# New tables for the attention loop and the MLP's list of a fused transformer block

## The chip, the cores and the metric

The kernel runs on one core of a Trainium2 chip. The core has TensorE (PE, with its weight loads as PEld), VectorE (DVE), ScalarE (ACT), GpSimd (POOL), and SyncE (SP), which here only issues transfers; sixteen DMA engines move the data. The metric is the device time of one launch in microseconds (us). Each time comes from several launches; one further launch is profiled.

## The reference

One block of a conditioned transformer, on 2048 tokens of width 640. A condition vector gives six modulation vectors (shift `s`, scale `c`, gate `g`, for two halves of the block). Everything is fp32.

```
mod = silu(c) @ w_mod                       # 6 vectors of 640
h = layernorm(x) * (1 + ca) + sa
q, k, v = h @ wqkv                          # 32 heads of 20
scores = q @ k.T * 20**-0.5                 # a query sees its own and the 255 tokens before
x = x + ga * (softmax(scores) @ v) @ wo
h = layernorm(x) * (1 + cb) + sb
x = x + gb * (gelu(layernorm(h) @ w1 + b1) @ w2 + b2)    # 640 -> 1536 -> 640
```

## The kernel before

**Splits.** Nearly every operand of a large product is held as a high and a low part (`hi`, `lo`), and a product of two of them is three matmuls: hi x hi, hi x lo, lo x hi. The high part is a rounding copy, the low part the difference of the value and its high part. Each copy and each difference is an instruction on DVE, ACT or POOL, and the tables say on which.

**Three stages.** A prologue normalizes the first 1024 tokens and makes the first q and k. Then comes a loop of steps `t`, 0 to 143, in which attention is computed while the remaining projections (q, k, v of the other heads and tokens) run beside it as filler for TensorE. Then comes the MLP with the output projection `wo` and the second and third layernorm of each group of 128 tokens (`bg`, 0 to 15), written as one explicit list.

**A step of the loop.** A quad is four heads; there are 8 quads and two halves of 1024 tokens, 16 in all, of 8 query blocks each. Step `t` computes the scores `s` of one query block (for their row maxima only), and, 11 steps later in the loop, `e`: the scores once more, transposed, with the maxima subtracted inside the product. DVE masks `e` and `s` and takes the maximum (`nm`); ACT takes the exponential of `e` (`pt`), POOL masks `pt`; two steps later TensorE multiplies `pt` with v (`o`), and ACT copies the result (`oT`). The maxima of a quad are turned and split at step 8k (`m_rows`: a transpose `pm`, two ACT instructions `mt` and `mhi`, one POOL difference `mlo`) and stored by SP as two rows each (`mhi`, `mlo`) into `qbuf`; `e` needs them from step 8k + 3 on. So rows written at step 64 are needed at step 67, those of step 80 at 83, and those of step 88 at 91.

**Four slots.** Behind the scores and the exponential each step has four slots, h = 0 to 3; a time like 64.25 means step 64, slot 1. All engines get their instructions in the order of the program. SP is one queue: a transfer that waits for a buffer, for data or for an earlier transfer to land holds up all transfers behind it.

**What fills the slots.** A unit is one q, k or v product of 128 features and 512 tokens: 15 matmuls, then an evacuation of hi and low part (or a copy of v and its four transposes, called an aside, since it needs a bank of its own). `UNITS` orders the units. `lay_units` spreads their matmuls over the steps, some 7.35 a step, with `EXTRA[t]` more or fewer at step t, and `LEAST` 4 at least while a unit lasts. `LOV` lists the units whose low part goes to DVE instead of POOL. `EARLY` and `AFTER` move the weight splits and the asides of a unit. A finished unit's q or k is written to DRAM by SP in the next step (`rows_out`: `q_scr`, `k_scr`), and read back for a quad into `qbuf` and `kbuf` by `rows_in`, not before two steps behind its last unit. Then there are, as time intervals: `MODS` for the modulation vectors of the second half (five loads `wm`, five additions on DVE), `WOS` for the output weights (`wor` loads, splits), `RS` for the sums of the softmax (a load `rd`, a reciprocal on DVE, a store `r_scr`), `LNS` and `HIA` for the layernorm of the tokens of the second half, `W1S` and `LATE_AT` for the first MLP weights and the last v, and `PREP`, `PREPS`, `PREPE`, `AHEAD` for splitting the MLP weights. For the latter, a load of 128 x 640 is issued `AHEAD` steps before, at `PREP` ACT makes the high part, a slot later the engine of `PREPE` the low part, and `PREPS` steps after `PREP` SP stores both.

`SUMS_LAST` lists steps in which the copy of `o` comes behind the exponential, `WHOLE` steps in which the maximum is one instruction instead of two. `WARM` puts matmuls without a use into a few steps. `TAIL_AT`, `TAIL0`, `PER` place the first token groups of the output projection into the last steps.

**The MLP's list.** `PLAN` is a list of words. A number n stands for the next n groups of three matmuls; each other word is a named operation, of `ops`. `w2hj` loads the w2 tile of step j into one of three buffers (`W2B`), `ghj` and `gl_j` split the activation, `load.Na`, `load.Nb` and `load.Nc` load attention output, reciprocal sums and x of token group N, `xrcm` loads a residual, `xbcm` adds its bias, `clcm` closes an output tile, `stcm` stores it, `a..`, `b..`, `e..` are sums and gelus of the first product. A residual load `xr` takes the buffer of a stored tile, so it waits until that store has landed. `MOVE` names the engine of each copy and difference of the list: `d` DVE, `a` ACT, `p` POOL.

The evacuation of rows, and the reading back, in the loop:

```python
                    for kind in range(2):
                        t = max([t, due - 8 * NSLOT + LAG + 8] + [over_at.get((kind, j, c2), -9) + 2 for j in js])
                        put(max(t, 0), 3, lambda half=half, quad=quad, kind=kind, c2=c2: rows_in(half, quad, kind, c2))
```

and the weights of the MLP:

```python
            later(at, lambda: nc.scalar.copy(hi, src))
            later(at + 0.25, lambda: e.tensor_tensor(lo, src, f32(hi), ALU.subtract))
            later(at + hold, store)
```

Of the kernel before, what the change touches and what calls it, by code (L numbers as in the profile page):

```python
# [99 lines left out]
e201 xr02 y1.4a 1 sa1.5a gh1 y1.4b 1 sa1.5b xr03 y1l.4 sa1.5c m0.5 w00.6 gl_1 load.7c x0.5a m1.5 w01.6 1 xr04 om.7  # L100
w02.6 1 sb0.5 sb1.5a w03.6 sr00 1 sb1.5b sb1.5c oh.7 rd.8 w04.6 x0.5b 1 ol.7 add0.6 n2.5 x1.5a sa0.6 1 xb00 x1.5b
p102 w10.6 xs.5 xb01 load.8a y0.5a 1 load.8c xb02 w11.6 y0.5b xb03 1 y0l.5 w12.6 raw.5a y1.5a xb04 1 t1.5 y1.5b
y1l.5 w13.6 raw.5b 1 t1h.5 w14.6 ri.8a t3.5 1 add1.6 1 ri.8b t1l.5 t2.5 x0.6a sa1.6a 1 a202 w00.7 x0.6b w2h4 e202 1
t2h.5 sa1.6b t4.5 load.8b sa1.6c gh2 w01.7 m0.6 1 gl_2 w02.7 m1.6 p103 x1.6a w03.7 load.9a w04.7 t2l.5 1 add0.7 1
sb0.6 om.8 w10.7 1 sa0.7 oh.8 w11.7 load.9b sb1.6a 1 x1.6b sb1.6b ol.8 xs.6 w12.7 1 w13.7 om.9 sb1.6c load.9c v000 1
a203 load.10b w14.7 e203 1 z000 add1.7 n2.6 1 sa1.7a oh.9 k000 w00.8 gh3 w2h5 y0.6a ol.9 gl_3 w01.8 1 y0.6b load.10a
sa1.7b y0l.6 w02.8 k100 1 sa1.7c raw.6a w03.8 k200 k300 t1.6 v100 1 k400 p104 w04.8 t1h.6 1 add0.8 t1l.6 y1.6a w10.8
z100 1 m0.7 w11.8 1 y1.6b m1.7 w12.8 y1l.6 1 sb0.7 raw.6b sb1.7a x0.7a a204 1 x0.7b sb1.7b w13.8 e204 v200 sb1.7c
sa0.8 1 z200 w14.8 n2.7 gh4 1 ss00 t3.6 gl_4 sr01 add1.8 x1.7a 1 om.10 x1.7b w2h6 y0.7a xs.7 t2.6 1 y0.7b load.10c
sa1.8a w00.9 load.11b p105 y0l.7 1 oh.10 sa1.8b t2h.6 y1.7a sa1.8c raw.7a 1 m0.8 t4.6 w01.9 t1.7 1 t2l.6 w02.9 y1.7b  # L110
t1h.7 m1.8 1 t1l.7 w03.9 y1l.7 1 sb0.8 raw.7b sb1.8a w04.9 a205 v001 1 t3.7 sb1.8b e205 add0.9 1 z001 t2.7 gh5 w10.9
1 sb1.8c th00 t2h.7 w11.9 w2h7 t2l.7 t4.7 w12.9 n2.8 k201 1 gl_5 sa0.9 th01 w13.9 ol.10 1 tl00 w14.9 a600 1 load.11a
add1.9 1 sa1.9a w00.10 sa1.9b 1 sa1.9c w01.10 k001 1 om.11 tl01 w02.10 1 oh.11 rd.12 w03.10 1 w04.10 1 k101 a700 1
add0.10 ol.11 1 b500 w10.10 a500 e500 1 k301 v101 load.11c w11.10 1 k401 z101 v201 w12.10 1 ri.12a z201 w13.10 a400
ri.12b 1 sr02 e400 w14.10 1 ss01 gh6 add1.10 1 gl_6 load.12b w00.11 a300 1 e300 w01.11 w2h8 1 v002 w02.11 z002 1
w03.11 k002 k202 a601 1 k102 w04.11 v102 k302 1 add0.11 1 k402 w10.11 z102 1 w11.11 1 v202 w12.11 z202 1 ss02 w13.11
sr03 a701 1 b501 w14.11 a501 1 e501 add1.11 4 a401 1 e401 1 gh7 1 a301 gl_7 1 e301 1 w2h9 v003 1 z003 1 a602 k203 1
k003 1 k103 1 v103 k303 1 z103 k403 2 a702 1 v203 b502 1 z203 a502 e502 2 ss03 sr04 1 a402 1 e402 1 gh8 1 gl_8 1
a302 1 e302 w2h10 2 a603 4 v004 z004 2 a703 1 k004 b503 k104 1 a503 e503 1 k304 k204 1 k404 v104 1 a403 v204 z104 1
z204 e403 1 gh9 1 a303 sr05 1 gl_9 e303 1 ss04 w2h11 2 a604 2 v005 1 z005 1 k005 k205 k105 1 k305 1 v105 k405 a704 1  # L120
z105 v205 1 b504 1 a504 z205 e504 2 a404 ss05 1 e404 1 gh10 1 a304 w1h10 gl_10 w1h11 1 e304 1 w2h12 2 a605 6 a705 1
b505 1 a505 e505 3 a405 1 e405 1 gh11 1 a305 w1h12 w1h13 1 gl_11 e305 x0.8a w2h13 gh12 1 x0.8b gl_12 1 cl00 x1.8a 1
x1.8b load.12a cl01 xs.8 y0.8a cl02 1 st00 y0.8b st01 1 y0l.8 st02 cl03 1 w2h14 gh13 y1.8a st03 cl04 1 y1.8b m0.9 1
# [1726 lines left out]
```

## Time and profile before

| | us |
|---|---|
| median of 3 runs | 974.69 |
| lowest, highest | 973.71, 974.96 |
| the profiled execution | 974.81 |
| its span, first to last instruction | 973.1 |

The profile lists busy time by engine, the granted clock of TensorE, the transfers, and for each instruction the idle time of its engine just before it with what ended it (its releaser). In a row of a timeline the first number is the start, the second the duration of the rows merged in it, both in us; `x3` counts them. In a view of waits the numbers are total us, times, and the longest. In a table of windows each engine has its busy time and its number of instructions, in the order PE, PEld, DVE, ACT, POOL; behind them stand the granted clock, the share of the DMA engines' time in use, and GB/s. `out<-in` names what an instruction writes and reads. Times in the views count from the start of the span.

### The profile page before, as it was taken

How to read it: one execution, taken by the hardware profiler on the slowest of the kernel's cores; microseconds unless marked ns; L12 is line 12 of the kernel's file. 1: busy time of each engine (PE TensorE's matmuls, PEld its weight loads, DVE VectorE, ACT ScalarE, POOL GpSimd, SP SyncE). 2: the span in 40 equal slices, each digit the busy share in tenths (PEclk: the TensorE clock that was granted, in tenths of full speed). 3: DMA queues.
4: the chain of work that ended last, by engine and by line, in shares of the span. 5: the costliest groups of instructions: out<-in, count | busy, mean ns of one | idle time of the engine just before them, and what ended most of it. 6: DMA issues, size and time to landing. Idle time of an engine off the chain costs nothing. (4 is left out here: it accounts for less than half of the span.)

```text
span 973.1 us, 20083 instructions
## 1 busy us (share of the span) xinstructions
PE 937.3 (96%) x7693; PEld 739.0 (76%) x7693; DVE 656.9 (68%) x1099; ACT 416.3 (43%) x738; POOL 491.8 (51%) x662
## 2 busy tenths in 40 slices
...
GB/s 309 96 213 214 295 289 324 267 224 264 264 310 264 228 278 218 288 118 149 215 165 171 80 88 332 172 190 173 206 245 274 278 165 244 210 169 180 97 288 162
DMA packets 109039, 212.01 MB, mean 218 GB/s; under 512 B 9840, under 2 KB 43088, under 8 KB 107408
## 3 DMA queue, kind: packets, MB, share of 16 engines
...
q8 instruction: 61, 1.00, 0.4%
...
## 5 line engine op out<-in xcount | busy, mean ns | idle before, releaser
L191 POOL TENSOR_SCALAR_AFFINE_SELECT pt<-pt 128x512 f32<-128x512 f32 x192 | 132.0, 687 | 126.9 <-ACT pt L191 115.0
L191 PE MATMUL out<-ghi,w 128*128 128x512 f32 x480 | 170.8, 397 | 1.8 <-DMA w<-w_scr 1.8
L191 ACT ACTIVATE pt<-e 128x1024 f32<-128x1024 f32 (+1 forms) x120 | 133.8, 1115 | 62.8 <-DVE e L191 62.0
L191 DVE TENSOR_REDUCE nm<-s 128x1 f32<-128x256 f32 (+4 forms) x193 | 156.8, 841 | 4.4
L191 PE MATMUL e<-qbuf,kbuf 62*128 62x128 f32 (+2 forms) x773 | 112.9, 330 | 14.6 <-ACT pt L191 9.7
L191 PEld LDWEIGHTS e<-qbuf,kbuf 62*128 62x128 f32 x773 | 80.9, 186 | 54.1 <-ACT pt L191 28.0
L191 PE MATMUL pp<-hhi,w_hi 128*128 128x512 f32 x265 | 115.3, 435 | 0.1
L191 DVE COPY_PREDICATED e<-mask_t,e 128x512 f32<-128x512 uint32 x96 | 66.6, 693 | 68.4 <-PE e L191 61.3
L191 PE MATMUL s<-kbuf,qbuf 60*128 60x256 f32 (+2 forms) x728 | 107.3, 304 | 4.0 <-DVE nm L191 1.5
L191 PE MATMUL pp<-hlo,w_hi 128*128 128x512 f32 x265 | 108.5, 410 | 1.3 <-POOL hlo L191 1.3
L191 PE MATMUL pp<-hhi,w_lo 128*128 128x512 f32 x265 | 105.6, 399 | 0.0
L191 PEld LDWEIGHTS out<-ghi,w 128*128 128x128 f32 x480 | 90.3, 188 | 19.2 <-ACT ghi L191 2.0
L191 PE MATMUL o<-pt,vbuf 128*32 128x128 f32 x2688 | 100.9, 279 | 0.0
L191 PEld LDWEIGHTS s<-kbuf,qbuf 60*128 60x128 f32 x728 | 88.3, 187 | 13.9 <-DVE nm L191 5.7
L191 PE MATMUL out<-glo,w 128*128 128x512 f32 x240 | 94.1, 392 | 0.2 <-DVE glo L191 0.2
L191 PE MATMUL P<-yhi,w1s 128*128 128x512 f32 x264 | 89.3, 391 | 1.1 <-DVE u L191 1.1
L191 DVE COPY_PREDICATED s<-mask_t,s 128x512 f32<-128x512 uint32 x112 | 77.1, 689 | 15.1 <-PE s L191 14.8
L191 POOL TENSOR_TENSOR w_lo<-wraw,w_hi 128x128 fp32r<-128x128 f32 (+1 forms) x166 | 75.8, 488 | 20.8 <-ACT w_hi L191 20.8
L191 ACT COPY oT<-o 128x128 f32<-128x128 f32 x128 | 33.9, 265 | 121.1 <-PE o L191 117.8
L191 PEld LDWEIGHTS o<-pt,vbuf 128*32 128x32 f32 x2688 | 67.7, 110 | 15.6 <-issue 3.1
L191 PEld LDWEIGHTS pp<-hhi,w_hi 128*128 128x128 f32 x265 | 49.9, 188 | 21.8 <-issue 12.3
L191 PE MATMUL wo<-wo_h,ot_hi 128*128 128x320 f32 x256 | 62.3, 326 | 0.1
...
## 6 DMA issues: line engine op xcount, KB each, us to landing
...
```

The lines of the kernel that those rows point to most:

```text
L191: return self.tc.keep_in_program_order(op(*args, **kw))
```

## The change

All lists of numbers named above are replaced, and nothing else: no function, shape, buffer or product changes. In the loop's tables:

```diff
-UNITS = ((0, ...), (1, 'q10', 'k00', 'q00', 'k10', 'q01', 'k11', 'k01', 'q11', 'v0', ...))
+UNITS = ((0, ...), (1, 'q10', 'k00', 'q00', 'k10', 'q01', 'k01', 'k11', 'q11', 'v0', ...))
-LNS = [-10.25, -3.75, -1.0, -1.5, 0.75, -0.5, 0.0]
-LOV = [1, 8, 12, 17, 18, 23, 24, 25, 35, 37, 43, 44, 47, 52, 55]
-HIA = [0, 1, 4, 5, 6, 7]
+LNS = [-10.75, -3.75, -1.0, -1.5, 0.75, -1.0, 0.0]
+LOV = [1, 8, 15, 17, 18, 24, 25, 28, 31, 35, 37, 43, 44, 47, 52, 55]
+HIA = [1, 2, 3, 5, 6, 7, 9]
-MODS = [[8.5, 18.25], [18.5, 27.25], [69.75, 79.0], [58.25, 67.25]]
-WOS = [86.5, 93.25, 98.75, 108.5, 111.75, 114.5, 118.5]
-W1S = [124.25, 122.25]
-RS = [[78.75, 80.5], [82.5, 86.75]]
+MODS = [[8.75, 18.75], [19.0, 27.25], [66.75, 77.25], [56.25, 65.25]]
+WOS = [86.0, 93.25, 98.25, 108.5, 111.75, 113.75, 117.5]
+W1S = [126.0, 121.5]
+RS = [[78.75, 80.25], [82.5, 84.75]]
-WARM = {(135, 0): 3, (136, 0): 4, (114, 3): 8, (120, 3): 1}
+WARM = {(135, 0): 2, (136, 0): 1, (114, 3): 8}
-PREP = [10.25, 14.5, 16.5, 25.0, 26.75, 29.25, 38.25, 39.75, 42.0, 49.75, 52.5, 54.5, 63.75, 65.5, 67.5, 75.0, 77.0, 78.5]
-PREPS = [0.75, 2.0, 1.5, 1.5, 1.5, 0.75, 1.0, 1.75, 2.0, 1.5, 1.5, 2.0, 1.5, 2.5, 0.5, 1.25, 2.0, 1.75]
-PREPE = 'ppppppppdpdppppppp'
-AHEAD = 4.0
+PREP = [9.0, 15.5, 16.25, 24.0, 26.75, 29.0, 38.0, 39.75, 41.75, 49.5, 52.25, 54.25, 64.25, 66.25, 67.25, 74.5, 77.25, 78.5]
+PREPS = [0.5, 1.75, 1.75, 1.75, 1.5, 0.5, 1.25, 1.75, 2.0, 1.5, 1.5, 2.0, 1.5, 2.0, 0.5, 1.25, 2.5, 1.75]
+PREPE = 'pppppddddppppppppp'
+AHEAD = 5.25
```

`EXTRA` has new values for about half of its steps. Worked out through `lay_units`, the products of a step change in 30 of 100 steps, mostly by one or two; the larger ones are step 21 (3 to 13), step 22 (15 to 2), step 33 (7 to 11), step 29 (10 to 8) and steps 47 and 48 (6 and 5 to 4 and 7). `EARLY` changes for 15 units, `AFTER` moves the asides of v1 to steps 74 and 75 (from 73 and 74), of v2 and v3 to 98 and 102 (from 97 and 101) and of the modulation vectors by one to three steps. `SUMS_LAST` loses four steps and gains five, `WHOLE` loses five and gains seven. `TAIL_AT` and `LATE_AT` change in single entries by a quarter step or so.

`PLAN` is written anew in the part where token groups and the first products run together, and nearly word for word the same where only MLP products are left. An example, the stretch at the last chunk of 512 tokens:

```diff
-w2h37 1 gh36 cl20 1 gl_36 cl21 st20 1 cl22 st21 1 cl23 st22 1 cl24 w2h38 gh37 st23 1 gl_37 st24 1 xr30 1 xr31 1 xr32 1 w2h39 gh38 1 gl_38 1 xr33 2 xr34 1 xb30 w2h40
+w2h37 1 gh36 cl20 1 gl_36 st20 1 cl21 1 cl22 st21 1 cl23 w2h38 st22 1 cl24 st23 1 gh37 st24 gl_37 1 xr30 1 xr31 1 gh38 w2h39 1 gl_38 2 xr32 1 xr33 1 gh39 w2h40 xr34
```

`MOVE` names another engine for 153 of its 326 words, for instance:

```diff
-'gh5': 'a', 'oh.6': 'p', 'gh14': 'p', 'v000': 'a', 'k102': 'p', 'gh36': 'a', 'gl_36': 'p'
+'gh5': 'a', 'oh.6': 'd', 'gh14': 'd', 'v000': 'p', 'k102': 'd', 'gh36': 'a', 'gl_36': 'd'
```

More of the change, by code (lines that the diff above doesn't have):

```diff
@@ new lines @@
+AFTER = {0: 1, 4: 3, 5: 2, 6: 1, 7: 1, 8: 1, 9: 1, 10: 2, 11: 1, 12: 3, 14: 1, 15: 3, 20: 1, 21: 1, 22: 1, 23: 3, 32: 1, 34: 2, 35: 1, 36: 1, 38: 1, 39: 3, 40: 4, 43: 2, 1: 1, 57: 2, 50: 4, 37: 1, 46: 2, 29: 1, 3: 1, 41: 1, 53: 2, 51: 2, 56: 2, 13: 1, 58: 3, 49: 1, 54: 1, 16: 1, 44: 1, 59: 1, 2: 1}
+SUMS_LAST = [14, 18, 23, 25, 26, 29, 33, 34, 42, 46, 59, 61, 64, 79, 80, 83, 85, 87, 88, 91, 92, 94, 100, 101, 105, 106, 107, 109, 110, 117, 121, 122, 123, 126, 128, 129, 130, 132, 133, 134, 135, 136, 137]
@@ L69 @@
-WOS = [86.5, 93.25, 98.75, 108.5, 111.75, 114.5, 118.5]
-W1S = [124.25, 122.25]
-RS = [[78.75, 80.5], [82.5, 86.75]]
+MODS = [[8.75, 18.75], [19.0, 27.25], [66.75, 77.25], [56.25, 65.25]]
+WOS = [86.0, 93.25, 98.25, 108.5, 111.75, 113.75, 117.5]
+W1S = [126.0, 121.5]
+RS = [[78.75, 80.25], [82.5, 84.75]]
 TOMID = 109
-WARM = {(135, 0): 3, (136, 0): 4, (114, 3): 8, (120, 3): 1}
-LATE_AT = [106.25, 106.25, 106.75, 108.5, 110.75, 111, 113.75]
+WARM = {(135, 0): 2, (136, 0): 1, (114, 3): 8}
+LATE_AT = [106.25, 106.5, 106.75, 108.5, 110.75, 111, 113.5]
@@ L100 @@
[L100 to L123, printed above, removed]
-st04 1 gl_13 m1.9 2 om.12 w2h15 gh14 1 sb0.9 load.13b sb1.9a oh.12 1 gl_14 xr10 1 ol.12 xr11 1 sb1.9b xr12 y1l.8
@@ L150 @@
-a715 1 b515 1 a515 e515 3 a415 1 e415 1 gh35 1 gl_35 1 a315 1 e315 w2h37 1 gh36 cl20 1 gl_36 cl21 st20 1 cl22 st21 1
-cl23 st22 1 cl24 w2h38 gh37 st23 1 gl_37 st24 1 xr30 1 xr31 1 xr32 1 w2h39 gh38 1 gl_38 1 xr33 2 xr34 1 xb30 w2h40 1
-gh39 xb31 1 gl_39 xb32 3 gh40 w2h41 1 xb33 gl_40 1 xb34 3 gh41 w2h42 1 gl_41 4 w2h43 gh42 1 gl_42 4 w2h44 gh43 1
-gl_43 4 gh44 w2h45 1 gl_44 4 gh45 w2h46 1 gl_45 4 gh46 w2h47 1 gl_46 4 gh47 1 gl_47 5 cl30 1 cl31 st30 1 cl32 st31 1
-cl33 st32 cl34 st33 st34
+load.6a w1h02 w2h1 w2h2 w2h3 w1h03 1 load.6b 1 m0.4 1 p100 x0.4a oh.5 1 m1.4 ol.5 1 x0.4b sb0.4 1 sb1.4a w1h04 x1.4a
@@ new lines @@
+ra00 1 ra01 w00.5 w01.5 x1.4b sb1.4b w02.5 p101 w03.5 a200 1 e200 w04.5 1 gh0 sb1.4c add0.5 1 sa0.5 gl_0 n2.4 w10.5
+w11.5 w12.5 w1h05 om.6 a201 y0.4a load.6c 1 load.7a y0.4b e201 xs.4 y0l.4 w13.5 xr00 1 oh.6 gh1 load.7b xr01 y1.4a 1
+ol.6 xr02 y1.4b y1l.4 w14.5 1 add1.5 gl_1 xr03 1 sa1.5a sa1.5b w00.6 m0.5 x0.5a sa1.5c w01.6 load.7c 1 m1.5 w02.6
+sr00 1 sb0.5 w03.6 sb1.5a 1 p102 xr04 sb1.5b w04.6 x0.5b sb1.5c 1 add0.6 xb00 om.7 x1.5a sa0.6 1 n2.5 load.8a w10.6
+x1.5b 1 xb01 xs.5 rd.8 y0.5a oh.7 w11.6 y0.5b 1 ol.7 xb02 y0l.5 w12.6 xb03 a202 y1.5a w13.6 raw.5a e202 load.8c 1
@@ new lines @@
+y1.5b t1.5 gh2 w14.6 y1l.5 1 raw.5b xb04 1 gl_2 t1h.5 add1.6 1 w2h4 t1l.5 w00.7 x0.6a t3.5 w01.7 ri.8a x0.6b 1
+sa1.6a x1.6a ri.8b w02.7 p103 t2.5 1 x1.6b sa1.6b xs.6 m0.6 w03.7 sa1.6c 1 t4.5 w04.7 load.9a 1 t2h.5 load.8b m1.6 1
+t2l.5 1 add0.7 sb0.6 w10.7 sb1.6a 1 v000 sa0.7 sb1.6b w11.7 z000 a203 1 om.8 e203 sb1.6c w12.7 1 gh3 k000 load.9b
+oh.8 k100 w13.7 w2h5 gl_3 1 n2.6 w14.7 1 ol.8 add1.7 y0.6a sa1.7a 1 om.9 k200 1 load.9c sa1.7b w00.8 load.10b y0.6b
+oh.9 v100 p104 w01.8 y0l.6 w02.8 sa1.7c ol.9 1 k300 raw.6a w03.8 load.10a y1.6a w04.8 k400 z100 1 t1.6 1 y1.6b m0.7
@@ new lines @@
+1 v200 1 add0.8 1 m1.7 w10.8 w2h6 y1l.6 w11.8 sb0.7 raw.6b x0.7a sb1.7a w12.8 a204 x0.7b t3.6 w13.8 sb1.7b w14.8
+e204 sa0.8 sb1.7c 1 z200 gh4 add1.8 x1.7a t2.6 1 ss00 n2.7 x1.7b sa1.8a load.10c gl_4 w00.9 om.10 xs.7 p105 y0.7a
+sr01 t2h.6 w01.9 y0.7b w02.9 1 y0l.7 oh.10 load.11b w03.9 sa1.8b raw.7a sa1.8c y1.7a ol.10 1 y1.7b t1.7 w04.9 m0.8
+load.11a 1 t1h.7 1 t1l.7 y1l.7 m1.8 1 raw.7b 1 add0.9 sb0.8 1 t3.7 sb1.8a w10.9 t1h.6 1 th00 t2.7 t1l.6 a205 w11.9
+w2h7 t2h.7 sb1.8b t4.7 w12.9 t2l.6 e205 w13.9 sb1.8c t2l.7 w14.9 gh5 t4.6 1 sa0.9 th01 gl_5 add1.9 1 tl00 n2.8
@@ new lines @@
+w00.10 tl01 1 w01.10 a600 1 sa1.9a w02.10 sa1.9b 1 w03.10 om.11 1 w04.10 1 add0.10 v001 oh.11 rd.12 1 sa1.9c ol.11
+w10.10 a700 1 a500 w11.10 z001 1 b500 load.11c ri.12a w12.10 e500 k001 1 k201 ri.12b w13.10 k101 1 v101 w14.10 k301
+z101 1 add1.10 k401 1 load.12b w00.11 1 a400 v201 w01.11 e400 z201 1 gh6 w02.11 a300 1 sr02 gl_6 e300 w03.11 ss01 1
+w04.11 w2h8 1 add0.11 1 w10.11 a601 1 v002 w11.11 z002 1 k002 k202 w12.11 k102 1 v102 k302 w13.11 1 z102 k402 w14.11
+2 add1.11 v202 1 a701 z202 1 a501 1 b501 sr03 1 e501 1 ss02 1 a401 1 e401 1 gh7 1 gl_7 1 a301 v003 1 z003 e301 w2h9
@@ new lines @@
+1 cl00 x1.8a 1 x1.8b load.12a cl01 xs.8 y0.8a 1 cl02 st00 y0.8b st01 1 y0l.8 st02 cl03 1 gh13 w2h14 cl04 y1.8a st03
+1 gl_13 st04 1 m0.9 1 y1.8b m1.9 2 y1l.8 w2h15 om.12 x0.9a 1 sb0.9 load.13b oh.12 sb1.9a 1 x0.9b ol.12 sb1.9b xr10 1
+sa0.10 sa1.10a x1.9a xr11 1 gh14 x1.9b sb1.9c xs.9 w00.12 sa1.10b w2h16 w01.12 w02.12 gl_14 n2.9 w03.12 w04.12 gh15
+y0.9a xr12 1 sa1.10c y0.9b load.12c gl_15 1 y0l.9 load.13a 1 y1.9a 1 m0.10 1 xr13 y1.9b xr14 m1.10 1 xb10 w2h17 1
+gh16 xb11 sb0.10 gl_16 1 sb1.10a y1l.9 1 sb1.10b sa0.11 sb1.10c x0.10a sa1.11a 1 x0.10b sa1.11b sa1.11c 1 n2.10
@@ new lines @@
+w2h18 gh17 x1.10a 1 xb12 x1.10b load.13c gl_17 xs.10 y0.10a add0.12 1 y0.10b w10.12 y0l.10 1 om.13 y1.10a xb13
+w11.12 m0.11 1 y1.10b xb14 oh.13 load.14b w12.12 w2h19 y1l.10 w13.12 m1.11 x0.11a gh18 w14.12 1 sb0.11 add1.12 ol.13
+1 sb1.11a sa0.12 1 sb1.11b sa1.12a 1 gl_18 load.14a sa1.12b w00.13 1 sb1.11c x0.11b w01.13 gh19 w2h20 sa1.12c 1
+n2.11 gl_19 w02.13 1 x1.11a 1 x1.11b load.14c xs.11 w03.13 om.14 1 load.15b oh.14 w04.13 1 add0.13 ol.14 y0.11a gh20
+w2h21 1 y0.11b w10.13 load.15a 1 y0l.11 gl_20 y1.11a w11.13 y1.11b m0.12 1 ra10 w12.13 y1l.11 1 m1.12 w13.13 1
@@ new lines @@
+w14.13 gh21 w2h22 ra11 1 add1.13 x0.12a sb0.12 1 x0.12b sa0.13 w00.14 sa1.13a sb1.12a 1 sb1.12b x1.12a gl_21 sa1.13b
+1 x1.12b xs.12 w01.14 1 sa1.13c sb1.12c w02.14 gh22 w2h23 1 gl_22 om.15 n2.12 w03.14 1 w04.14 1 oh.15 add0.14 y0.12a
+1 ol.15 y0.12b w10.14 y0l.12 1 load.15c w11.14 gh23 w2h24 1 gl_23 w12.14 1 w13.14 1 w14.14 1 add1.14 y1.12a 1 y1.12b
+m0.13 w00.15 w2h25 y1l.12 1 m1.13 w01.15 x0.13a sb0.13 1 sb1.13a x0.13b sa0.14 w02.15 sb1.13b p110 sa1.14a 1 sb1.13c
+sa1.14b w03.15 cl10 sa1.14c 1 n2.13 st10 w04.15 cl11 1 add0.15 st11 x1.13a 1 x1.13b xs.13 y0.13a 1 y0.13b w10.15
@@ new lines @@
+6 a712 1 a512 1 b512 1 e512 2 a412 1 e412 1 gh32 1 a312 sh14 gl_32 1 e312 1 w2h34 2 a613 6 a713 1 a513 1 b513 1 e513
+2 a413 1 e413 1 gh33 1 a313 sh15 gl_33 1 e313 1 w2h35 2 a614 6 a714 1 a514 1 b514 1 e514 2 a414 1 e414 1 gh34 1 a314
+gl_34 1 e314 1 w2h36 2 a615 6 a715 1 a515 1 b515 1 e515 2 a415 1 e415 1 gh35 1 gl_35 1 a315 1 e315 w2h37 1 gh36 cl20
+1 gl_36 st20 1 cl21 1 cl22 st21 1 cl23 w2h38 st22 1 cl24 st23 1 gh37 st24 gl_37 1 xr30 1 xr31 1 gh38 w2h39 1 gl_38 2
+xr32 1 xr33 1 gh39 w2h40 xr34 1 gl_39 xb30 1 xb31 3 gh40 w2h41 1 xb32 gl_40 1 xb33 3 gh41 w2h42 xb34 1 gl_41 4 gh42
```

59 lines of the change are left out of this document (23 added, 36 removed).

## The prediction

> **What bounds the kernel now.** The page's busy table comes first, then busy time by stage.
>
> ```profile
> PE 937.3 (96%) x7693; PEld 739.0 (76%) x7693; DVE 656.9 (68%) x1099; ACT 416.3 (43%) x738; POOL 491.8 (51%) x662
> ```
> ```profile
> 50.00:500.00 450.00, 437.28 (x4600) 324.70 (x4600) 334.99 (x464) 249.62 (x472) 274.11 (x404) 1.00 0.78 241
> 500.00:600.00 100.00, 90.63 (x1080) 72.53 (x1081) 77.44 (x133) 48.89 (x86) 57.42 (x73) 0.97 0.51 158
> 600.00:900.00 300.00, 297.33 (x1449) 247.27 (x1448) 196.26 (x365) 78.03 (x123) 125.02 (x141) 1.00 0.62 213
> 900.00:973.10 73.10, 67.24 (x295) 54.74 (x293) 18.17 (x28) 13.05 (x20) 14.06 (x13) 1.00 0.53 183
> ```
>
> TensorE is the bound. After the start it idles 12.7 us in the loop of 128 score steps (450.00 - 437.28), 9.4 us where attention runs out, 2.7 us in the MLP's middle and 5.9 us at the end. The tables move work and take none of it away, so they can win only these idles, and what a lowered clock costs beside them. The view of waits, for PE alone, names who ended them:
>
> ```profile
> PE e L191 <- ACT pt L191: 9.7, 15, 2.0
> PE e L191 <- DMA qbuf<-mlo: 3.4, 3, 2.1
> PE out L191 <- DMA w<-w_scr: 1.8, 2, 1.6
> ```
>
> Two of the three are transfers, 5.2 us together. The timeline of PE gives the places, the longest first (idle before the row and its releaser in brackets):
>
> ```profile
> 304.08 0.40 PE L191 MATMUL pp<-hhi,w_lo 128*128 128x512 f32 x1
> 304.31 0.40 PE L191 MATMUL pp<-hhi,w_hi 128*128 128x512 f32 x1
> 306.83 0.77 PE L191 MATMUL e<-qbuf,kbuf 62*128 62x256 f32 x3 [2.12 <-DMA qbuf<-mlo]
> ```
>
> The wait at 306.83 costs more than its 2.12 us. Busy time in short windows, the granted clock third from the end:
>
> ```profile
> 300.00:306.80 6.80, 4.71 (x43) 3.14 (x41) 5.14 (x7) 2.82 (x4) 3.32 (x3) 1.00 0.96 318
> 307.50:310.30 2.80, 2.80 (x35) 2.07 (x33) 1.86 (x3) 0.18 (x2) 0.00 (x0) 0.50 1.01 352
> 311.00:316.00 5.00, 5.00 (x59) 3.72 (x58) 2.61 (x5) 3.76 (x9) 3.78 (x5) 1.00 0.20 78
> 938.00:942.00 4.00, 3.84 (x17) 3.20 (x18) 0.00 (x0) 1.44 (x3) 1.17 (x1) 1.00 0.72 285
> ```
>
> Behind it the clock is 0.50 for at least 2.80 us (307.50 to 310.30) and at most 4.2 (306.80 to 311.00). Half of that is lost: 1.4 to 2.1 us. Behind the wait at 938 (below) it stays 1.00.
>
> **The row transfers (step 67).** mhi and mlo are the rows of score maxima of one quad, written at step 64 and needed by e at step 67. SP's issues ahead of the late one:
>
> ```profile
> 295.93 0.33 SPq L191 DMA_DIRECT2D prep<-in_w  x1
> 298.29 1.13 SPq L191 DMA_DIRECT2D kbuf<-k_scr  x2
> 299.47 0.39 SPq L191 DMA_DIRECT2D wraw<-in_wqkv  x1
> 299.90 0.94 SPq L191 DMA_DIRECT2D q_scr<-stage  x2
> 300.94 0.53 SPq L191 DMA_DIRECT2D qbuf<-mhi  x1
> 301.74 1.35 SPq L191 DMA_DIRECT2D qbuf<-mlo  x1
> ```
>
> Sizes follow from shapes: a row transfer 32 x 128 floats, 16 KB; each kbuf 60 x 2 x 512, 240 KB; a prep load 128 x 640, 320 KB, its store twice that; xr 128 x 512, 256 KB. mlo's 16 KB hold e until 306.83, 5.1 us after the issue began, while the DMA share is 0.96: it stands behind what was issued just before. UNITS swaps k1's and k0's second chunk, so quad 0's k0 is complete at step 59 instead of 61 and the kbuf pair goes out at step 61 instead of 63. There SP waits for k0's write to land, with step 62's k_scr writes queued behind it; nothing of these is due before step 64, so 0. AHEAD 5.25 moves the prep load from 63.5 to 62.0. That takes 800 KB out of the run-up; at 318 GB/s, 2.6 us. PREP 64.25 also puts prep's low part on POOL behind mlo instead of ahead of it:
>
> ```profile
> L191 POOL TENSOR_TENSOR prep<-prep 128x640 fp32r<-128x640 f32 x16 | 25.6, 1598 | 10.8 <-ACT prep L191 10.8
> ```
>
> so mlo itself can be ready 1.6 us earlier. Of the 2.12 us the bytes alone cover all. I take the whole idle and 1.6 us of clock: **-3.7 us** (bounds 0 and -4.2).
> The Trainium skill (TensorE: Matmul & The Clock Gate, "Part 1: The HAM clock gate") says that the clock is halved after an idle window of about 3.4 us. By that rule 2.12 us would halve nothing, this term would be -2.1 and the time 971.0; the rows show the halving right behind 2.12 us, so I give the rule 0.02, inside the forecast's chance.
>
> **Step 91.** Here SP itself is late with the rows:
>
> ```profile
> 404.09 0.52 PE L191 MATMUL e<-qbuf,kbuf 62*128 62x128 f32 x5 [1.06 <-DMA qbuf<-mlo]
> ```
>
> ```profile
> 394.32 1.77 SPq L191 DMA_DIRECT2D kbuf<-k_scr  x2
> 396.19 0.58 SPq L191 DMA_DIRECT2D r_scr<-rd  x1
> 397.74 1.59 SPq L191 DMA_DIRECT2D q_scr<-stage  x2
> 399.42 0.58 SPq L191 DMA_DIRECT2D qbuf<-mhi  x1
> 401.47 0.55 SPq L191 DMA_DIRECT2D qbuf<-mlo  x1
> ```
>
> Before the kbuf pair stand four wor loads. WOS starts them half a step earlier (86.0) and RS stores r_scr two steps earlier (84.75). mlo is issued at 301.74 in step 64 and at 401.47 in step 88: 4.2 us a step, so half a step is some 2.1 us, an estimate. Against 1.06 us I take **-0.9** (0 to -1.1).
>
> **The last chunk.**
>
> ```profile
> 928.23 2.22 SPq L191 DMA_DIRECT2D xr<-x_scr  x3
> 930.50 0.44 SPq L191 DMA_DIRECT2D w<-w_scr  x1
> ```
> ```profile
> 938.16 0.47 PE L191 MATMUL out<-ghi,w 128*128 128x512 f32 x1 [1.63 <-DMA w<-w_scr]
> ```
>
> The w2 tile of 930.50 reaches its matmul at 938.16. Three residual loads are issued ahead of it; in the new list two are (xr32 follows w2h39), and w2h38 goes ahead of three stores instead of two. One xr less is 0.26 MB at the 285 GB/s around 938, 0.9 us, and its issue 0.7 us of 2.22. But cl21 to cl24 come one group later, and their stores free the buffers that xr waits for; and w2 has only three buffers, so its lead is unchanged from issue slot to use. Of 1.8 us I take **-1.3** (0 to -1.8).
>
> **Chains through DVE in the loop.**
>
> ```profile
> 181.96 0.38 PE L191 MATMUL s<-kbuf,qbuf 60*128 60x256 f32 x1 [0.65 <-DVE nm L191]
> ...
> 212.00 0.38 PE L191 MATMUL s<-kbuf,qbuf 60*128 60x256 f32 x1 [0.90 <-DVE nm L191]
> ...
> 342.77 0.44 PE L191 MATMUL e<-qbuf,kbuf 62*128 62x256 f32 x2 [0.66 <-ACT pt L191]
> ```
>
> A product costs 0.23 us (304.08 to 304.31). Step 33 gets 11 products for 7, 0.9 us of cover for the 0.65 at 181.96: -0.65. Step 75 gets 4 products and v1's four transposes for 5 products; I take a third of the 0.66 at 342.77: -0.2. Unit 23's low part goes from DVE to POOL, ahead of the late maximum at 212.00, but a prep low part comes to DVE at step 40; -0.4 of 0.90. Together **-1.25** (+1 to -2.2; plus, if DVE is the later one).
>
> **What it adds.** Step 22 keeps 2 products of 15 and no other filler, step 47 four of six. Counted from the tables, 27 steps of the old list have four or fewer, and the whole loop idles 12.7 us, so such a step costs some 0.5 us at the most; with two products less it is about +0.7, and I take **+0.7** for both (0 to +2.5). Of the `warm` fillers five go; PE waits for ACT right behind them, so 0. Were it not so, five at less than a product's 0.23 us would save up to 1.2, and what they cover would show as idle instead.
>
> **The rest has one answer.** TAIL0, PER and NEXT stay and the few TAIL_AT shifts fall in the same or the next quarter step, so I leave the 9.4 us between 500 and 600 as they are. PLAN keeps its 456 groups; six of its ten `load.Na` (o) go out 1.3 to 8.5 us of PE work earlier (products counted from word to word at 0.23 us), one 2.5 later, and 153 of 326 copies and differences change engine (DVE 141 to 132, POOL 115 to 121, ACT 70 to 73). In 600 to 900 PE idles 2.7 us; I cost the new order at 0, covered by the queue of products, and if that cover fails it is a new wait of the size of those 2.7. SUMS_LAST, WHOLE, HIA, AFTER, EARLY, MODS, W1S and LATE_AT move single instructions of under 1.6 us by a step or less. For waits that I can't see, from the loop's own 12.7 us idle with about a tenth rearranged, **+1.0** (-1 to +5).
>
> **Sum:** -3.7 - 0.9 - 1.3 - 1.25 + 0.7 + 1.0 = -5.45 us. The profiled execution took 974.8 us (span 973.1), 0.1 above the median of 974.7; 974.8 - 5.45 = **969.4 us**.
>
> **Rivals.**
> (a) The waits go, but the new order makes as many elsewhere: the 15 waits of e on exp are a matter of what precedes them on ACT and DVE, and both queues are rearranged. The idle of the 7.15 us that the first four terms win is lost again, without a halved clock: 974.8 - 1.6 + 0.7 = 973.9 us.
> (b) The change doesn't do what it says: the landing at step 67 is set by the q_scr stores right ahead of the rows, which stay. Then 3.7 of the gain is missing: 974.8 - 1.75 = 973.1, inside the same band or at its edge.
> (c) Slower: the bytes pile up at step 80 instead.
>
> ```profile
> 358.21 0.59 SPq L191 DMA_DIRECT2D w_scr<-prep  x1
> ```
> ```profile
> 363.40 0.56 SPq L191 DMA_DIRECT2D qbuf<-mlo  x1
> ```
> ```profile
> 370.18 0.55 PE L191 MATMUL e<-qbuf,kbuf 62*128 62x128 f32 x5 [0.22 <-ACT pt L191]
> ```
>
> This store (640 KB) moves from step 79.0 to 79.75, closer to the rows: up to 0.66 MB at 318 GB/s, 2.1 us more ahead of mlo. It has 6.8 us until 370.18, and took up to 5.1 at step 67; it decides from 1.7 us on. If it is late by 2 us as at step 67, the idle and the clock cost 3.7 us, and where the same bytes have not left step 67's run-up either, 973.1 + 3.7 = 976.8 us. Against it: at step 80 no kbuf pair stands in those seconds between.
> The Trainium skill (DMA: Bandwidth & Descriptors, "Queues, rings and completion order") says that each DMA engine consumes one issuer's descriptors in ring order; by that rule only what is issued ahead of mlo delays it, which is what (c) needs and the late 16 KB at step 67 agree with.
>
> **How the numbers follow.** Forecast 0.66, (a) 0.17, (b) 0.05, (c) 0.12. What a measurement can tell from no change is about 0.2%, 1.9 us: 972.8 to 976.6. The forecast lies below it for most of its bounds; (a) and (b) lie in it, (c) above. Faster 0.66, same 0.21, slower 0.13. With the four gains at their lower bounds the sum is -9.3 + 1.7 and the time 967; without the unseen +1.0 it is 966; the range reaches from there to just under (c): 966.0 to 976.5.
>
> **What would show it.** The rows at 306.83 and 404.09 without idle by DMA, one stretch of clock 0.50 fewer, kbuf's pair two steps before mhi, 1.8 us less wait of out on w. Wrong would be: the row wait at another quad, PE's waits on ACT above 12 us, or idle in 600 to 900 well above 2.7 us.

## The result and the profile after

The changed kernel takes 964.17 us (median of 4, 962.88 to 965.25) beside 974.83 us (973.71 to 976.08) for the kernel before in the same measurement: ratio 0.989, 95% interval 0.9872 to 0.9908, or 10.7 us less. Measured again beside the experiments it is 0.9906 (0.9878 to 0.9933). The forecast was 969.4 us with a range from 966.0; the sign came, the gain is twice the forecast and lies below the range.

The profiled execution after took 962.88 us (span 961.1), 12.0 us of span less than before. Its busy table:

```profile
PE 931.0 (97%) x7683; PEld 736.9 (77%) x7683; DVE 651.6 (68%) x1091; ACT 418.9 (44%) x741; POOL 496.7 (52%) x669
```

Busy time by stage, columns as before (stretch, its length, then busy time and count for PE, PEld, DVE, ACT, POOL, then clock, DMA share and GB/s):

```profile
50.00:500.00 450.00, 440.70 (x4647) 327.09 (x4646) 341.90 (x470) 251.79 (x474) 272.43 (x407) 1.00 0.78 244
500.00:600.00 100.00, 90.09 (x1055) 72.27 (x1054) 77.34 (x139) 46.32 (x82) 57.77 (x72) 0.98 0.56 175
600.00:900.00 300.00, 299.88 (x1469) 253.04 (x1469) 182.44 (x339) 85.88 (x135) 138.94 (x152) 1.00 0.61 209
900.00:961.10 61.10, 56.09 (x245) 45.24 (x243) 20.02 (x33) 8.13 (x12) 6.45 (x5) 1.00 0.57 193
```

The loop idles 9.3 us instead of 12.7, the end of attention 9.9 instead of 9.4, the MLP's middle 0.1 instead of 2.7. But the row of the middle says more than its idle: 1469 matmuls in 300 us where there were 1449. Twenty products at 0.23 us would be 4.6 us; the idle fell by 2.55.

The waits of PE, summed:

```profile
PE e L191 <- ACT pt L191: 10.1, 18, 2.0
...
PE out L191 <- DMA w<-w_scr: 1.1, 2, 0.8
```

The transfers' waits for the rows are no longer among the large ones, and the two for w2 lost 0.7 us. To see where the 12 us went, three marks of the same work serve: the mask of the scores at steps 64 and 127, on DVE, and the end. Before:

```profile
295.39 0.68 DVE L191 COPY_PREDICATED s<-mask_t,s 128x512 f32<-128x512 uint32 x1
...
543.15 0.68 DVE L191 COPY_PREDICATED s<-mask_t,s 128x512 f32<-128x512 uint32 x1
```

After:

```profile
297.42 0.68 DVE L191 COPY_PREDICATED s<-mask_t,s 128x512 f32<-128x512 uint32 x1
...
538.55 0.68 DVE L191 COPY_PREDICATED s<-mask_t,s 128x512 f32<-128x512 uint32 x1
```

Up to step 64 the changed kernel is 2.0 us later; from there to step 127 it wins 6.6 us (247.8 to 241.1), and from step 127 to the end of the span another 7.4 us (429.95 to 422.55). The last stretch, where I had put -1.3 us, is the larger half.

In the middle stretch the wait at step 67 is gone. The timeline of PE there, after:

```profile
306.12 0.40 PE L191 MATMUL pp<-hhi,w_lo 128*128 128x512 f32 x1
306.35 1.17 PE L191 MATMUL pmc<-ones,acc 128*128 128x1 f32 x10
307.38 0.48 PE L191 MATMUL pp<-hhi,w_hi 128*128 128x512 f32 x1
307.79 0.56 PE L191 MATMUL e<-qbuf,kbuf 62*128 62x256 f32 x3
```

No idle stands before e. Ten small products pmc, of the conditioning (MODS), stand ahead of it, which in the kernel before came later. The clock in windows, after:

```profile
307.50:310.30 2.80, 2.80 (x41) 2.14 (x41) 2.08 (x5) 0.56 (x2) 0.70 (x1) 1.00 0.99 326
521.40:524.90 3.50, 3.06 (x43) 2.46 (x40) 3.39 (x5) 1.77 (x3) 2.53 (x4) 1.00 0.67 187
551.70:555.00 3.30, 3.30 (x14) 2.93 (x15) 1.83 (x3) 1.93 (x2) 0.00 (x0) 0.50 0.12 40
```

Before, the second of these places was halved too:

```profile
525.50:528.70 3.20, 3.20 (x34) 2.53 (x32) 2.90 (x4) 1.33 (x1) 2.46 (x4) 0.50 0.94 246
```

The stretch at 307 went with its wait, as forecast. The one at 525 also went, though the wait ahead of it stayed: 1.50 us at 523.99 before, 1.49 us at 519.93 after. That needs an explanation of its own (last section), and 1.7 of the 6.6 us won between steps 64 and 127 belong to no table then.

### The profile page after: what moved, and what is told of

It is laid out like the page before. It is cut to its first block, busy times and chain, and to the rows that moved or that the text cites. A ratio compares the mean times of both kernels' runs of the same rounds, so it can differ in the third digit from the quotient of the medians.

```text
span 961.1 us, 20078 instructions
## 1 busy us (share of the span) xinstructions
PE 931.0 (97%) x7683; PEld 736.9 (77%) x7683; DVE 651.6 (68%) x1091; ACT 418.9 (44%) x741; POOL 496.7 (52%) x669
## 5 line engine op out<-in xcount | busy, mean ns | idle before, releaser
L191 POOL TENSOR_SCALAR_AFFINE_SELECT pt<-pt 128x512 f32<-128x512 f32 x192 | 132.1, 688 | 125.9 <-ACT pt L191 119.0
L191 PE MATMUL out<-ghi,w 128*128 128x512 f32 x480 | 168.8, 395 | 1.1 <-DMA w<-w_scr 1.1
L191 ACT ACTIVATE pt<-e 128x1024 f32<-128x1024 f32 (+1 forms) x120 | 133.8, 1115 | 66.1 <-DVE e L191 61.9
L191 DVE TENSOR_REDUCE nm<-s 128x4 f32<-128x1024 f32 (+4 forms) x191 | 156.7, 848 | 4.4
L191 PE MATMUL e<-qbuf,kbuf 62*128 62x128 f32 (+2 forms) x773 | 112.9, 329 | 11.5 <-ACT pt L191 10.1
L191 PEld LDWEIGHTS e<-qbuf,kbuf 62*128 62x128 f32 x773 | 80.2, 186 | 50.6 <-ACT pt L191 26.6
L191 PE MATMUL pp<-hhi,w_hi 128*128 128x512 f32 x265 | 114.9, 433 | 1.0 <-ACT w_hi L191 0.9
L191 DVE COPY_PREDICATED e<-mask_t,e 128x512 f32<-128x512 uint32 x96 | 66.5, 693 | 64.8 <-PE e L191 55.9
L191 PE MATMUL s<-kbuf,qbuf 60*128 60x256 f32 (+2 forms) x728 | 106.9, 304 | 3.3 <-DVE stage L191 1.4
L191 PE MATMUL pp<-hlo,w_hi 128*128 128x512 f32 x265 | 108.1, 408 | 0.6 <-POOL hlo L191 0.6
L191 PE MATMUL pp<-hhi,w_lo 128*128 128x512 f32 x265 | 105.8, 399 | 0.0
L191 PEld LDWEIGHTS out<-ghi,w 128*128 128x128 f32 x480 | 90.2, 188 | 19.1 <-issue 2.3
L191 PE MATMUL o<-pt,vbuf 128*32 128x128 f32 x2688 | 99.5, 277 | 0.2 <-ACT vbuf L191 0.2
L191 PEld LDWEIGHTS s<-kbuf,qbuf 60*128 60x128 f32 x728 | 86.8, 186 | 14.1 <-DVE nm L191 5.5
L191 PE MATMUL out<-glo,w 128*128 128x512 f32 x240 | 93.9, 391 | 0.0
L191 POOL TENSOR_TENSOR w_lo<-wraw,w_hi 128x128 fp32r<-128x128 f32 x171 | 76.9, 481 | 23.2 <-ACT w_hi L191 21.4
L191 DVE COPY_PREDICATED s<-mask_t,s 128x512 f32<-128x512 uint32 x112 | 77.1, 689 | 16.9 <-PE s L191 16.9
L191 PE MATMUL P<-yhi,w1s 128*128 128x512 f32 x264 | 88.3, 390 | 0.1
L191 ACT COPY oT<-o 128x128 f32<-128x128 f32 x128 | 33.8, 264 | 108.0 <-PE o L191 107.7
L191 PEld LDWEIGHTS o<-pt,vbuf 128*32 128x32 f32 x2688 | 66.9, 109 | 15.5 <-issue 1.9
L191 PEld LDWEIGHTS pp<-hhi,w_hi 128*128 128x128 f32 x265 | 49.9, 188 | 22.3 <-issue 10.0
L191 PE MATMUL wo<-wo_h,ot_hi 128*128 128x320 f32 x256 | 61.3, 323 | 0.1
```

Of the source, the lines that this page charges most:

```text
L191: return self.tc.keep_in_program_order(op(*args, **kw))
```

## The experiments

The first theory (A): the loop's tables bring about what was forecast, and the new order of the MLP's list, which I had costed at nothing, brings the rest. The rival (B): the list is worth nothing, and what was won behind step 127 is clock and what the loop handed on. Each ratio below is to the kernel before on the same chip, whose median there was 972.4 to 973.7 us.

### List and loop apart

mlp_new is the kernel before with these two tables new, loop_new the changed kernel with these two old:

```diff
-MOVE = {'p100': 'a', 'oh.5': 'd', 'ol.5': 'p', 'x0.4b': 'a', 'ra00': 'd', 'x1.4b': 'a',
+MOVE = {'p100': 'a', 'oh.5': 'd', 'ol.5': 'p', 'x0.4b': 'd', 'ra00': 'd', 'ra01': 'p',
...
 PLAN = """
...
```

> The kernel before with PLAN and MOVE alone made new; all tables of the loop stay old. Theory A (the step of the prediction that failed is the new order of the MLP costed at 0): start-to-start times of the products in 600 to 850 lose some 5.4 us of stall, more than the idle that the view shows there (2.7 us), and the last chunk waits 0.7 us less, so -5 to -7 us: 968 to 970 us, with idle in 600 to 900 near 0. Rival B (the order is worth nothing, what was won behind step 127 is the clock stretch at 525 and what the loop handed on): within 1.5 us of before, 973 to 975.

> The kernel after with the old PLAN and the old MOVE; all tables of the loop are new. Theory A: the loop's gain up to step 127, 4.6 us, and the clock stretch behind 525 if that belongs to the loop, 1.7 us: 968 to 970.5 us, and the idle of 600 to 900 is back (2.7 us). Rival B: nearly all of the gain, 964 to 966 us.

mlp_new: 967.38 us, 0.9934 (0.9913 to 0.9955), -6.4 us. loop_new: 971.45 us, 0.9983 (0.9963 to 1.0002). Theory A holds for the list; the loop's part is smaller than A had it. Busy time from the MLP's first product to the last, the same 1820 matmuls, in the kernel before:

```profile
585.40:969.05 383.65, 379.08 (x1820) 314.42 (x1819) 224.97 (x413) 97.34 (x152) 150.91 (x163) 1.00 0.61 211
```

and in mlp_new:

```profile
584.40:961.66 377.26, 375.17 (x1820) 315.64 (x1819) 217.21 (x404) 99.69 (x155) 160.70 (x169) 1.00 0.63 215
```

6.4 us shorter at full clock. The other profiles of this study agree: in seven with the new list whole this stretch takes 376.8 to 377.4 us, in three with the old list and no half-clock window inside it (this one, units, units_prep) 383.2 to 383.8. Idle fell from 4.57 to 2.09 us, 2.5 us; the other 3.9 us were counted as busy. Three rows of PE's timeline in the kernel before show how:

```profile
691.72 0.39 PE L191 MATMUL out<-glo,w 128*128 128x512 f32 x1
691.95 0.39 PE L191 MATMUL out<-ghi,w 128*128 128x512 f32 x1
692.85 0.50 PE L191 MATMUL P<-yhi,w1s 128*128 128x512 f32 x1 [0.51 <-DVE u L191]
```

A product lasts 0.39 us in the view, but the next one starts 0.23 us after it (691.72 to 691.95). From 691.95 to 692.85 is 0.90 us, so 0.67 us were lost where 0.51 is shown, and a wait under 0.16 us leaves no idle at all. From the intervals between starts, the MLP before has 66 over 0.3 us, mlp_new 46. What all intervals exceed 0.23 us by sums to 12.7 us before and 7.2 in mlp_new, so 5.5 of the 6.4 us show there.

### Order and engines apart

plan has the new PLAN alone, move the new MOVE alone. after_again is the changed kernel once more, and few the kernel before with nine tables new: PLAN, MOVE, UNITS, AHEAD, PREP, PREPS, PREPE, WOS and RS, of which the short ones are

```diff
-AHEAD = 4.0
+AHEAD = 5.25
...
-WOS = [86.5, 93.25, 98.75, 108.5, 111.75, 114.5, 118.5]
+WOS = [86.0, 93.25, 98.25, 108.5, 111.75, 113.75, 117.5]
...
-RS = [[78.75, 80.5], [82.5, 86.75]]
+RS = [[78.75, 80.25], [82.5, 84.75]]
...
```

> The changed kernel once more, so that all parts are measured beside it on one chip. If the parts add up, PLAN with MOVE (-6.4 us, 0.9934) and the loop's tables (-1.6 us, 0.9983) give 0.992; the first measurement gave 0.989 with an interval of 0.9872 to 0.9908, 2.7 us more than the parts. Theory A (parts add up, the rest is scatter of the half-clock stretches): 0.990 to 0.993. Rival (the two parts help each other): 0.987 to 0.989.

> The kernel before with the new PLAN and the old MOVE: the order of the MLP's words alone, the engines as before. If the order does it: -4.5 to -6.5 us and M's 800th product some 5 us earlier. If order and engines were fitted to each other and work only together: slower than before or at most -2 us.

> The kernel before with the new MOVE and the old PLAN: 153 copies and differences on other engines, order as before. If the order does it: within 1.5 us of before. If the engines do it: -4 us or more. If both work only together: slower than before.

> The kernel before with new PLAN, MOVE, UNITS, AHEAD, PREP, PREPS, PREPE, WOS and RS; the other thirteen tables old. By the sum of the parts so far -6.4 (PLAN, MOVE) - 2.4 (UNITS with prep) - 0.9 (step 91): -9.7 us, 0.990. If the other thirteen tables bring a gain of their own, it is 1 us or more above the changed kernel; if they cost (their first 64 steps are 2.0 us longer in the trace), as fast as it or up to 2 us faster.

plan: 1.0 (0.9982 to 1.0019). move: 1.0115 (1.008 to 1.0149), 13 us slower by the medians. Together -6.4. So neither has a price of its own. In move PE waits where the list of before had room, the view of waits from 580 on:

```profile
PE wo L191 <- DVE xb L191: 5.7, 6, 2.0
PE wo L191 <- POOL ot_lo L191: 2.0, 2, 1.5
```

after_again: 0.9906, within the interval of the first measurement; that is 9.1 us, and the parts mlp_new and loop_new sum to 8.0, within the intervals, so nothing speaks for a gain that only the two together have. few: 0.9918 (0.9892 to 0.9943), as fast within the intervals.

### Which words of the list

The two lists hold the same 993 words and can be cut where both have done the same words and the same 456 entries of products. list_a takes words 1 to 461 new, list_b 462 to 841, list_c the rest, each with its engines.

```diff
-load.6a w2h1 w1h02 w2h2 w2h3 w1h03 load.6b 2 m0.4 1 p100 x0.4a oh.5 1 m1.4 ol.5 x0.4b 1 ra00 w1h04 x1.4a 1 x1.4b 1
+load.6a w1h02 w2h1 w2h2 w2h3 w1h03 1 load.6b 1 m0.4 1 p100 x0.4a oh.5 1 m1.4 ol.5 1 x0.4b sb0.4 1 sb1.4a w1h04 x1.4a
...
```

> The kernel before; the first 461 words of PLAN with their engines of MOVE new, up to the word a405 (some 480 of the MLP's 1368 products), the rest of list and engines old. In the trace with both new the 500th product comes 3.2 us earlier, counted from step 127. If the gain lies along the whole list and each stretch carries its own part: -3 us (970 to 971 beside 973). If list and engines work only as a whole: no gain or slower.

> The kernel before; words 462 to 841 of PLAN (after a405, up to gl_28) with their engines new, first and last part old. By the trace with both new, from the 480th to the 822nd product: -2 us. If list and engines work only as a whole: no gain or slower.

> The kernel before; only the words from w2h30 on (with the last chunk's loads and stores) and their engines new. By the prediction's term for the last chunk -1.3 us; by the trace with both new -1.2 us, of which the shown idle for w is the smaller part. Rival: the w2 waits stay where they are and the time is that of before.

| kernel | ratio (95%) | MLP's first product to the last, us | to before |
|---|---|---|---|
| list_a | 0.9986 (0.9975 to 0.9997) | 379.98 | -3.7 |
| list_b | 0.9967 (0.9952 to 0.9982) | 381.00 | -2.6 |
| list_c | 1.0011 (0.9996 to 1.0026) | 382.74 | -0.9 |
| mlp_new | 0.9934 (0.9913 to 0.9955) | 377.26 | -6.4 |

By the length of the MLP each stretch carries its part, as long as its order and engines are new together; the sum of the three is 7.2. The times are no proof of that: they sum to -3.5 us, with intervals of 1.1 to 1.5 us on either side of each, and the clock differs (list_a's ten executions have a mean granted clock of 0.9922, list_b's 0.9942, the kernel before 0.9938 there). list_c's 0.9 us does not show in its time, and its last chunk still waits (its list is broken into lines elsewhere, so the view's L201 is L191 of the others):

```profile
939.29 0.47 PE L201 MATMUL out<-ghi,w 128*128 128x512 f32 x1 [1.46 <-DMA w<-w_scr]
```

Then one group of words. In the kernel before, DVE waits for the weight sums that ACT and POOL make; the view of waits for DVE, 600 to 900:

```profile
DVE w1s L191 <- ACT w1s L191: 5.9, 2, 3.7
...
DVE wr L191 <- POOL w1s L191: 3.9, 1, 3.9
DVE w1s L191 <- POOL w1s L191: 3.8, 1, 3.8
```

13.6 us together, with the sums u that PE needs behind them in the program. In the changed kernel POOL waits for DVE instead (POOL's view, same stretch):

```profile
POOL wr L191 <- DVE w1s L191: 22.2, 3, 9.1
```

wsum gives 30 of these words their new engines, wlist gives all 78 words of the weight sums their new places and engines:

```diff
-'v000': 'a', 'k200': 'd', 'v200': 'd', 'v001': 'a', 'k301': 'p', 'z101': 'd',
+'v000': 'p', 'k200': 'p', 'v200': 'p', 'v001': 'p', 'k301': 'd', 'z101': 'p',
...
```

> The kernel before with new engines for 30 of the weight sums' words (k, v, z) alone, order as before. If VectorE's stalls on those words hold up the sums that TensorE waits for (u at 692.85 and 718.26, 1.46 us from start to start): both waits gone, the MLP from its first product to the end 382.2 us instead of 383.6. If engines without their places only move the stall: the same 383.6 or longer.

> The kernel before with the 78 words of the weight sums (sr, k, v, z, ss) at their new places in the list, counted in products ahead of them, and on their new engines; all other words as before. If these words carry the gain of the first part: 380 to 381 us from the MLP's first product to the end, -2.5 to -3.5 us. If the list and its engines count as a whole: 383 us or more.

Both are slower: 1.0023 (1.0007 to 1.004) and 1.0026 (1.0013 to 1.0038), with 385.86 and 386.46 us for the MLP. In wsum the two waits for u are gone, but PE waits elsewhere:

```profile
PE wo L191 <- DVE xb L191: 1.5, 1, 1.5
PE out L191 <- POOL glo L191: 1.4, 3, 0.8
PE out L191 <- ACT ghi L191: 1.4, 1, 1.4
```

In wsum DVE also still waits 7.7 us for weight sums of ACT and POOL. So this group alone is not the cause; no other group was tried. The gain belongs to the list and the engines fitted to each other, stretch by stretch.

### Step 67

```diff
...
-'q01', 'k11', 'k01',
+'q01', 'k01', 'k11',
...
```

> The kernel before with k11 and k01 changed places in UNITS alone: the kbuf pair (480 KB) goes out two steps earlier, prep's load and its low part stay where they were. By the bytes ahead of mlo at 318 GB/s 1.5 us of the 2.12 us idle at step 67 go and the half-clock stretch with them: -1.5 to -3.2 us, 971.5 to 973.3. Rival (the landing is set by the q_scr stores right ahead, or by POOL's low part): wait and stretch stay, 974 to 975.

> The same change of places, and AHEAD, PREP, PREPS and PREPE new. By the prediction's term the whole wait at step 67 and its stretch of half clock go: -3.7 us, 971.0. If the swap alone suffices, the same as that kernel within 0.5 us. Rival (the row wait comes back at step 80, since prep's store moves to 79.75): idle of e by DMA at another quad of 1 us or more, 973 or above.

units: 0.9991 (0.9973 to 1.0008). units_prep: 0.9976 (0.9963 to 0.9989), -2.4 us, 971.32 where 971.0 was expected; but that the time came is luck, for the wait that was to go is there. The swap by itself leaves it nearly whole; with the prep loads it is still 1.55 us. units, then units_prep:

```profile
306.29 0.53 PE L191 MATMUL e<-qbuf,kbuf 62*128 62x256 f32 x3 [1.80 <-DMA qbuf<-mlo]
```
```profile
307.33 0.53 PE L191 MATMUL e<-qbuf,kbuf 62*128 62x256 f32 x3 [1.55 <-DMA qbuf<-mlo]
```

The eight experiments that change the list alone (mlp_new, plan, move, list_a to list_c, wsum, wlist) run the old loop and give the scatter of this wait: with the kernel before nine profiled executions, 2.11 to 3.48 us, mean 2.5. So the moves took some 1.0 us of it. The halved clock behind it is less regular: five of these nine have a half-clock window behind the wait, and list_b, move, plan and wsum, with waits of 2.11 to 2.66 us, have none. What happened to the rest shows on SP, POOL and ACT in units_prep:

```profile
300.97 0.54 SPq L191 DMA_DIRECT2D qbuf<-mhi  x1
305.06 0.50 SPq L191 DMA_DIRECT2D qbuf<-mlo  x1
```
```profile
300.78 0.45 POOL L191 TENSOR_TENSOR mlo<-mt,mhi 32x128 fp32r<-32x128 f32 x1
```
```profile
298.44 0.33 ACTq L191 DMA_DIRECT2D o_scr<-oT  x1
```

mlo is ready at 301.23, and once issued it reaches e in 2.3 us instead of 5.1. But SP issues it only at 305.06: the trace shows it waiting on a semaphore (a counter that a landing transfer raises) that ACT's store of o_scr sets, the transfer issued at 298.44; its last update comes at 305.00. The bytes left the run-up as I had it; the wait moved ahead of the issue. Why that store takes 6.6 us stays open.

The other suspect was MODS, which I had put among the tables that cost nothing. few_mods adds it to few, after_mods takes it out of the changed kernel:

```diff
-MODS = [[8.5, 18.25], [18.5, 27.25], [69.75, 79.0], [58.25, 67.25]]
+MODS = [[8.75, 18.75], [19.0, 27.25], [66.75, 77.25], [56.25, 65.25]]
```

> The kernel few (new PLAN, MOVE, UNITS, AHEAD, PREP, PREPS, PREPE, WOS, RS) with MODS new as well, so that the conditioning products pmc stand ahead of e at step 67. If they cover the rest: the wait for the rows falls from 1.56 us to 0.4 or less, step 72 is reached 1.0 to 1.5 us earlier than in few, and the time is 964 us, 0.9895 to 0.9915 of before. Rival: the wait stays at 1.5 us and the time at that of few.

> The changed kernel with the old MODS. If the products that MODS moves are the cover at step 67: the wait for the rows is back with 0.8 us or more, and the kernel is 0.8 to 2.5 us slower than the changed one. Rival: no wait there, as in the changed kernel, since the other tables carry it.

few_mods: 962.85 us, 0.9902 (0.989 to 0.9915). The rows of e at step 67 in few, then in few_mods, where no idle of 0.2 us or more is left:

```profile
307.66 0.53 PE L191 MATMUL e<-qbuf,kbuf 62*128 62x256 f32 x3 [1.56 <-DMA qbuf<-mlo]
```
```profile
305.55 1.17 PE L191 MATMUL pmc<-ones,acc 128*128 128x1 f32 x10
306.58 0.48 PE L191 MATMUL pp<-hhi,w_hi 128*128 128x512 f32 x1
307.21 0.53 PE L191 MATMUL e<-qbuf,kbuf 62*128 62x256 f32 x3
```

after_mods: 0.9945 (0.9931 to 0.9959), and the wait is back:

```profile
306.67 0.53 PE L191 MATMUL e<-qbuf,kbuf 62*128 62x256 f32 x3 [0.80 <-DMA qbuf<-mlo]
```

Both directions agree on the wait: SP still issues mlo late (304.38 in few_mods, 304.44 in the changed kernel, 301.74 before), and the products pmc in front of e, 1.03 us from start to start (305.55 to 306.58), cover most of what was left. The times say less. The intervals of few and few_mods overlap. after_mods is 3.8 us slower than after_again by the ratios, where 0.8 to 2.5 us was expected; but its profile has two half-clock windows between steps 64 and 127, at 495.94 and 523.24, neither of them behind step 67, which cost 3.4 us, and the changed kernel's profiles have none there. few_mods is as fast as the changed kernel with ten of its 22 tables; nothing measured here says that the other twelve bring anything.

### The first 64 steps

mix is the changed kernel with the old entries up to step 62:

```diff
-        at = PREP[len(parts)] - AHEAD
+        at = PREP[len(parts)] - (4.0 if len(parts) < 12 else AHEAD)
...
```

> The changed kernel, but up to step 62 with the old tables (EXTRA, EARLY, LOV, AFTER, SUMS_LAST, WHOLE, the first two MODS, the first twelve preps with their load 4 steps ahead instead of 5.25). In its traces the changed kernel takes 2.0 us longer than before up to step 64. If that belongs to these entries: step 64 is reached 2 us earlier than in the changed kernel, -2 us on it, 0.988 to 0.989 of before. Rival: what they cost up to step 64 they give back later (products laid earlier leave less behind), so the time is that of the changed kernel, 0.9906.

mix: 0.994 (0.9923 to 0.9958). It is not faster than the changed kernel, and if anything slower than the rival had it. From the first product of the scores to the mask of step 64 it takes 247.5 us, the changed kernel 248.8 and 248.3 in its two profiles. But it arrives at the rows earlier, waits for them again although the products pmc stand ahead of e here too, and has the clock halved behind the wait:

```profile
307.65 0.53 PE L191 MATMUL e<-qbuf,kbuf 62*128 62x256 f32 x3 [0.86 <-DMA qbuf<-mlo]
```
```profile
308.90:312.00 3.10, 3.10 (x29) 2.35 (x22) 2.36 (x4) 1.80 (x3) 0.61 (x1) 0.50 1.03 270
```

## Why the prediction was wrong

**The step that failed** is "In 600 to 900 PE idles 2.7 us; I cost the new order at 0, covered by the queue of products", under "The rest has one answer". It rested on the opening claim that the tables "can win only these idles, and what a lowered clock costs beside them". Measured by mlp_new, PLAN and MOVE are worth -6.4 us, of which 2.5 us were idle in the view and 3.9 us stood inside rows counted as busy. The last chunk belongs to this list, so -6.4 stands in the place of the 0 and of the -1.3 together, and the sum would have been 964.3; the measurement is 964.2. That it fits so closely is in part luck. The terms of the loop, with the +1.0 for unseen waits, sum to -4.15; loop_new measures -1.6 (-3.6 to +0.2), and the changed kernel less mlp_new gives -2.7 to -4.3. None of the signs that the prediction named for being wrong came (no row wait at another quad, waits for exp of 10.1 us, 0.1 us of idle in 600 to 900): all of them stand for a smaller gain, none for a larger one. I had also looked at the 153 engine changes and the order as if each had its own price; alone they are worth 0 and +11 to +13 us.

**Step 67** (-3.7): in the two profiles of the prediction and the result the size came, idle and half clock both gone, but the reason was wrong, and the 1.6 us of clock was luck: only five of the nine executions with the old loop have it. "Of the 2.12 us the bytes alone cover all" does not hold: UNITS and PREP leave 1.55 us, and MODS, costed at nothing, covers most of the rest. Rival (b) was right that something behind these moves sets the landing, though the runs show an older transfer's semaphore ahead of the issue rather than the q_scr stores.

**Step 91** (-0.9): the wait is gone in every run with the new WOS and RS. In the nine executions of the old loop it was 1.07 us at the most, under 0.25 in five and 0.4 in the mean, so its worth was less than half of what one profile showed. units_prep, with the old WOS and RS, does not have it either, so it is not shown that these two tables took it away.

**The last chunk** (-1.3): not shown. 1.8 us became 1.07 in the profile after,

```profile
921.63 0.47 PE L191 MATMUL out<-ghi,w 128*128 128x512 f32 x1 [0.31 <-DMA w<-w_scr]
...
926.06 0.47 PE L191 MATMUL out<-ghi,w 128*128 128x512 f32 x1 [0.76 <-DMA w<-w_scr]
```

but this wait for w2 scatters. In the nine profiles with the old order of the last chunk it sums to 0 (units) to 2.07 us (list_b), 0.75 in the mean; in the nine with the new one to 0.75 to 1.46 us, 1.13 in the mean. So the new order does not shorten the wait, and the 1.8 us of one execution were no price for it. list_c's MLP is 0.9 us shorter than that of the kernel before; where that comes from is open.

**DVE chains** (-1.25): 0.65 gone, 0.90 became 0.59, 0.66 became 0.46: -1.2 us, as forecast, beside a new wait of 0.22 at 333.74. loop_new and after_again show the same within 0.02 us; no experiment took these apart.

**What it adds** (+0.7): 2.0 us up to step 64 in one pair of profiles; counted from the first product of the scores, 248.3 to 248.8 us in three with all new tables of the loop beside 246.4 to 247.9 in nine with the old ones, 1.6 us in the mean. Of it 0.4 to 1.2 us stand in the first eight steps of every run with the new PREP for them (units_prep and few among them; mix, with the old entries, has none), which I had not costed. mix shows that it could not simply be taken back.

**500 to 600**, forecast as it was: 9.4 and 9.9 us idle, right. **Rivals (a) and (c)** did not come: PE's waits for exp grew by 0.4 us only, and there is no wait for the rows at step 80.

What stays open: which waits of the MLP make up the 3.9 us that no row shows as idle. The experiments place them by stretch of the list, not by word.
